# Retention attention and two MLPs on one core: q, k and v loaded in five transfers a chunk, and three moves on ScalarE in the first MLP

## The chip, the core and the metric

The kernel runs on one core of a Trainium2 chip. A core has TensorE (PE) for matrix products, VectorE (DVE), ScalarE (ACT) and GpSimd (POOL) for elementwise work, and SyncE (SP), which here issues nearly all DMAs. The engines run side by side and wait for each other through semaphores; each engine takes its own instructions strictly in the order of the program. The metric is the device time of one execution in microseconds (us).

## The reference

Attention with decay over 2 batches and 8 heads of 768 positions by 64, in blocks, then two MLPs over the 1536 tokens. Everything is float32.

```
for b in range(nb):                                   # blocks of the sequence
    intra = (qb @ kb.T) * Dmask                       # lam**(i-j), j <= i
    out   = intra @ vb + (qb * lam_pow) @ kv_state
    kv_state = lam_block * kv_state + (kb * rev_pow).T @ vb
x = out as (1536 tokens, 512)
h = x @ w_in1 ; x = (h * cos(h)) @ w_out1             # w_in: 512 x 2048, w_out: 2048 x 512
h = x @ w_in2 ; out = (h * sigmoid(h)) @ w_out2
```

## The kernel before

All instructions stand in the order in which the code below is written; there is no scheduler. Four stages follow each other, and on PE they join without a break.

**Attention** works on 6 chunks (c) of 128 positions. Per chunk, `load_qkv` brings k, q and v of all 16 (batch, head) pairs into a tile of 128 partitions, one position a partition, 64 numbers (256 B) a head. Two heads at a time are transposed on PE (`transposed`, tiles `pt`), copied out by ACT (`kT`, `qT`), multiplied into scores (`psc`), masked by DVE with the table `dm` and multiplied with v (`pso`). In parallel k is decayed (`att_kdec`, `kd`, on POOL from chunk 1 on) for the state (`pkv`). For batch 1 the kernel wants an odd and an even head to stand in the other half of the 128 rows than for batch 0. Before, the load did this: batch 1 of k and q came in two strided transfers which put heads 1, 3, 5, 7 on even places and 0, 2, 4, 6 on odd ones. k and q tiles have 2 buffers, v has 3; chunk c+2 is requested while chunk c is worked on. Between them SP also loads the first weights.

**First MLP, `gemm_in_0`.** The tokens are split in a part A of 1024 tokens, computed by seven products (`product(A, 1)` to `product(A, 7)`, six matmuls each), and a part B of 512 tokens by a plain product (`plain`, twice 12 matmuls). 2048 hidden columns are done in 8 pairs j of 2 x 128. One pass of the loop over j holds, on PE in this order, products 1, 7, 6 and 2 of pair j, `plain(B, 0)` of pair j-1, product 5, `plain(B, 1)`, and products 3 and 4: 66 matmuls. Three PSUM banks of A are copied on the way by ACT: `copy_ab` (L462) after product 1 starts a second sum from the first, and product 6 needs it; `copy_u` (L469) saves the bank as `u2` after product 6 and as `u4` after product 5. Products 5 and 3 go on summing in the bank that `u2` and `u4` save, so product 3 can't start before the `u4` copy has read it.

The activation of a finished half (`source`) takes four steps: `act_n` on ACT (L485, number of turns), `act_s` on DVE (L494, remainder), `act_sin` on ACT (L501, the sine), `act_g` on DVE (L507, times h), and a store of the result to DRAM (`gd`) by SP. In pass j this is done for both halves of part A of pair j-1 (`old`) and for half 0 (the only one) of part B of pair j-1 (`Bq`).

The weights of pair j+1 are made ready in the same pass by tasks that are put into slots (j, 0), (j, 1) and (j, 2) of the loop. Weights come as 64-bit words in tiles `raw` (512 KB, 3 buffers). `rebias_w` (ACT, L109) reads one half of the words, `convert_w` (DVE, L118 and L119) the other; only after both is the buffer free and `load_next` has SP load the next piece into it. `sum_w` (POOL, L137, tiles `S`) forms sums of weight blocks, `split_plain` and `split_sums` split weights and sums into a rounded part (ACT, L124) and a rest (POOL, L125, `win`).

```
for i in range(2):
    put((j - 1, 0), lambda f=f + i: convert_w(0, f, 0), load_next)   # pair j, f = 2j
put((j - 1, 0), lambda j=j: sum_w(0, j, nc.gpsimd))
put((j - 1, 1 - early), lambda j=j: split_plain(0, j))
put((j - 1, 2 - early), lambda j=j: split_sums(0, j))
```

By this rule pass p converts pieces 2p+2 and 2p+3 and at once loads pieces 2p+5 and 2p+6; and pass p also rebiases pieces 2p+4 and 2p+5. The later of these two, 2p+5, is thus requested in the pass that rebiases it, behind its first `convert_w`.

**After the loop** PE goes on with `gemm_out`, which reads the stored `gd` back (`load_half`, `load_g`), splits it (`prepare_half`, `prepare`: ACT L124 `gh`, POOL L125 `gl`) and multiplies it with the second weights, `wout`. The second MLP repeats the pattern; the change does not touch it.

Of the kernel before, what the change touches and what calls it, by code (L numbers as in the profile page):

```python
# [8 lines left out]
F32 = mybir.dt.float32  # L9
# [31 lines left out]
def tile_decay_attention__two_mlps(  # L41
# [158 lines left out]
    ps_s, ps_o = (psum_up.enter_context(tc.tile_pool(name=n, bufs=1, space=PSUM)) for n in ("ps_s", "ps_o"))  # L200
    half = [slice(e * C, (e + 1) * C) for e in range(2)]

    ident = ap_c.tile([P, P], F32, name="ident")
    lamb = ap_c.tile([P, P], F32, name="lamb")[:, 0:H]
    dm = ap_c.tile([P, H, P], F32, name="dm")
    qp = ap_c.tile([P, B, NP, P], F32, name="qp")

    def scan(out, step, first):
        nc.vector.tensor_tensor_scan(out=out, data0=step, data1=first, initial=0.0, op0=ALU.mult, op1=ALU.add)

    def table_dm():
        step = stage.tile([P, H, P], F32, tag="raw", name="step")
        nc.vector.tensor_copy(step, lamb[:, :, None].to_broadcast([P, H, P]))
        nc.vector.memset(step[:, :, 0:1], 0.0)
        scan(*(t.rearrange("p h i -> p (h i)") for t in (dm, step, diag)))

    def table_qp():
        first, step = both[:, 0], both[:, 1]
        by_s = lamb.rearrange("p (s y) -> p y s", y=2)
        for y in range(2):  # L220
            for b in range(B):
                lam_y = by_s[half[y], y ^ b]
# [24 lines left out]
    def transposed(c, part, pt, b):  # L247
        for s in range(NP):
            nc.tensor.transpose(
                pt[:, b, s, :], qkv[c, part][:, b, 2 * s:2 * s + 2, :].rearrange("p h d -> p (h d)"), ident  # L250
            )
# [33 lines left out]
    def att_kdec(c):  # L285
        if c == SC - 1:
            return
        t = ap_k.tile([P, B, H, D], F32, tag="kd", name="kd")
        engine = nc.gpsimd if c else nc.vector
        engine.tensor_tensor(  # L290
            out=t[:, 0], in0=qkv[c, "k"][:, 0], in1=dm[:, :, P - 1:P].to_broadcast([P, H, D]), op=ALU.mult
        )
        for y in range(2):
            engine.tensor_tensor(
                out=t[:, 1, y::2], in0=qkv[c, "k"][:, 1, y::2], in1=dm[:, 1 - y::2, P - 1:P].to_broadcast([P, NP, D]), op=ALU.mult
            )
        kd[c] = t

    def att_kv(c, pool, tag):
        if c == SC - 1:  # L300
            return
        ps = pool.tile([P, B, NP, D], F32, tag=tag, name="pkv")
        kt, vt = kd.pop(c), qkv[c, "v"]
        for b in range(B):
            for s in range(NP):
                for r in range(2):
                    nc.tensor.matmul(ps[half[r], b, s, :], kt[:, b, 2 * s + r, :], vt[:, b, 2 * s + (b ^ r), :], start=True, stop=True)
        pkv[c] = ps

    def att_state(c):  # L310
# [13 lines left out]
    def att_scores(c, b, pool, tag):  # L324
        (qT, _), kT = tr[c, "q"], tr[c, "k"]
        if b == 0:
            at[c] = ap_2.tile([P, B, 2, NP, P], F32, tag="at", name="at", bufs=1)
        ps = [pool.tile([P, NP, P], F32, tag=tag, name="psc", bufs=3) for _ in range(2)]
        for s in range(NP):
            for r in range(2):  # L330
                nc.tensor.matmul(ps[r][:, s, :], kT[half[r], b, s, :], qT[half[r], b, s, :], start=True, stop=True)
        for r in range(2):
            nc.vector.tensor_tensor(out=at[c][:, b, r], in0=ps[r], in1=dm[:, (b ^ r)::2, :], op=ALU.mult)

    def att_inter(c, pool, tag):
        ps = pool.tile([P, B, NP, P], F32, tag=tag, name="pso")
        po[c] = ps
        _, qd = tr[c, "q"]
        if c == 0:
            return  # L340
        st = state.pop(c)
        for s in range(NP):
            for e in range(2):
                for b in range(B):
                    r = half[b ^ e]
                    nc.tensor.matmul(ps[half[e], b, s, :], st[r, b, s, :], qd[r, b, s, :], start=s == 0, stop=False, skip_group_check=True)

# [113 lines left out]
    def copy_ab(Q):  # L461
        nc.scalar.copy(Q.banks["b"], Q.banks["a"])  # L462
# [50 lines left out]
    def gemm_in_0(tasks):  # L513


        def task(j, i):
            for x in tasks.get((j, i), []):
                x()

        old = quads_a[0]  # L520
        for j in range(1, FP):
            A, Bq = quads_a[j], quads_b[j - 1]
            if j > 1:
                product(A, 1)
# [48 lines left out]
        act_sin(Bq, 0)  # L573
        act_g(Bq, 0)
        gemm_out(0, 0, 1, (0, 1))
        task(FP, 1)
        prepare(0, 0, 2)
# [244 lines left out]
                send(2, m)  # L822

    with tc.manual_schedule():
        nc.scalar.dma_start(out=lamb, in_=lam.partition_broadcast(P))
        load_qkv(0, "k")
        load_qkv(0, "q", nc.scalar)
        load_qkv(0, "v")
# [131 lines left out]
        for L in range(2):  # L960
            tasks = {}
            if L == 0:
                for j in range(2, FP):
                    f = 2 * j
                    if j > 2:
                        put((j - 2, 2), *(lambda f=f + i: rebias_w(0, f, 0) for i in range(2)))
                        for i in range(2):
                            put((j - 1, 0), lambda f=f + i: convert_w(0, f, 0), load_next)
                        put((j - 1, 0), lambda j=j: sum_w(0, j, nc.gpsimd))
                    early = j == 2  # L970
                    put((j - 1, 1 - early), lambda j=j: split_plain(0, j))
                    put((j - 1, 2 - early), lambda j=j: split_sums(0, j))
# [70 lines left out]
```

## Time and profile before

| | |
|---|---|
| median of 3 runs | 570.6 us (570.12 to 571.87) |
| the profiled execution | 570.55 us, of which the span in the trace is 568.8 us |
| PE busy | 555.7 us, 98% of the span |
| DVE, ACT, POOL busy | 353.4, 294.4, 337.3 us |
| granted PE clock | 0.999 of full speed |
| DMA | 97.02 MB, mean 171 GB/s |

PE is busy nearly all the time, so 13.1 us of the span are PE's idle time, and what matters is which waits PE has and where. 1.75 us lie outside the span. Times below are microseconds from the start of the span.

### The profile page before, as it was taken

To read this page: it belongs to the slowest core of one execution; us is meant where nothing else is said; L and a number is where in the kernel's file an instruction comes from. 1 tells how busy PE (TensorE), PEld (TensorE's weight loads), DVE (VectorE), ACT (ScalarE), POOL (GpSimd) and SP (SyncE) were. 2 spreads that over 40 slices of the span, in tenths; PEclk is the share of its full clock that TensorE was granted. 3 is DMA by queue.
4 is the path that set the end of the run, shared out by engine and by line. 5 is a ranking of instruction groups with operands and counts; after the bars stand their busy time and mean duration, and the time that the engine had idled before them with its cause. 6 is when DMAs were issued, how large, how long until landed. Compare 5 with 4: busy or idle time off the path is not lost.

```text
span 568.8 us, 8373 instructions
## 1 busy us (share of the span) xinstructions
PE 555.7 (98%) x3168; PEld 461.4 (81%) x3168; DVE 353.4 (62%) x365; ACT 294.4 (52%) x440; POOL 337.3 (59%) x251
## 2 busy tenths in 40 slices
PE   7999999999999999999999999999999999999997
PEld 5878788777778688888888889888888888888885
DVE  6688876677669699900897446666866899102001
ACT  5567486667777655411842476556657555101220
POOL 3688355444455799950575067556727799901441
PEclk9999999999999999999999999999999999999999
DMA  8999235554437976650332045555558986205501
GB/s 196 209 228 260 60 127 186 184 181 154 138 154 271 358 260 227 233 169 1 115 109 74 2 154 196 184 186 178 211 193 307 359 253 184 75 0 176 195 1 74
DMA packets 79656, 97.02 MB, mean 171 GB/s; under 512 B 40704, under 2 KB 57088, under 8 KB 79616
## 3 DMA queue, kind: packets, MB, share of 16 engines
q1 hardware_dynamic: 77376, 95.96, 51.9%
q10 hardware_dynamic: 2240, 0.53, 0.4%
q8 instruction: 25, 0.41, 0.3%
q14 instruction: 15, 0.12, 0.1%
HBM read 68.16 MB, written 28.31 MB: 170 GB/s over the span
## 4 chain that ended last, share of the span: by engine, by line
PE 74%; DVE 6%; ACT 5%; POOL 5%; DMA 4%; issue 4%; SPq 1%; ACTq 0%; POOLq 0%; DVEq 0%
PE cab L705 38%; PE cab L432 18%; PE d L705 7%; PE d L432 6%; DMA raw<-in_moe_w_in_dram 2%; DVE s L494 2%; DVE s L507 1%; POOL gl L125 1%; ACT w L109 1%; POOL S L137 1%; ACT s L485 1%; POOL xal L398 1%; PE pso L353 1%; PE cab L448 1%; DMA raw<-in_moe_w_out_dram 1%
## 5 line engine op out<-in xcount | busy, mean ns | idle before, releaser
L125 POOL TENSOR_TENSOR gl<-gf,gh 128x512 fp32r<-128x512 f32 (+1 forms) x68 | 127.4, 1881 | 87.3 <-ACT gh L124 59.1
L705 PE MATMUL cab<-gh,wout 128*128 128x512 f32 x320 | 98.6, 389 | 0.0
L705 PE MATMUL cab<-wout,gh 128*128 128x512 f32 x320 | 98.5, 389 | 0.0
L119 DVE SCALAR_TENSOR_TENSOR w<-w,sb 128x512 uint32<-128x512 uint32 x64 | 90.1, 1408 | 8.1 <-ACT w L109 1.7
L432 PE MATMUL cab<-xah,win 128*128 128x512 f32 x320 | 87.3, 394 | 3.3 <-ACT cab L462 3.3
L124 ACT CAST gh<-gf 128x512 fp32r<-128x512 f32 (+1 forms) x68 | 53.4, 792 | 65.1 <-DMA out_dram<-o 38.7
L432 PEld LDWEIGHTS cab<-xah,win 128*128 128x128 f32 x320 | 58.6, 188 | 17.1 <-ACT cab L462 5.8
L137 POOL TENSOR_TENSOR S<-w 128x256 f32<-128x256 f32 x26 | 27.2, 1048 | 73.2 <-DVE w L119 73.2
L705 PEld LDWEIGHTS cab<-gh,wout 128*128 128x128 f32 x320 | 60.1, 188 | 12.6
L705 PEld LDWEIGHTS cab<-wout,gh 128*128 128x128 f32 x320 | 59.9, 188 | 12.3
L125 POOL TENSOR_TENSOR wout<-w,wout 128x512 fp32r<-128x512 f32 x32 | 52.4, 1643 | 22.9 <-ACT wout L124 22.9
L705 PE MATMUL cab<-wout,gl 128*128 128x512 f32 x160 | 62.4, 390 | 0.0
L705 PE MATMUL cab<-gl,wout 128*128 128x512 f32 x160 | 62.2, 389 | 0.0
L118 DVE TENSOR_SCALAR sb<-raw 128x512 uint32<-128x512 uint32 x64 | 59.4, 928 | 3.1 <-DMA raw<-in_moe_w_out_dram 2.1
L432 PE MATMUL cab<-xal,win 128*128 128x512 f32 x160 | 49.4, 390 | 0.0
L780 DVE COPY o<-cab 128x512 f32<-128x512 f32 x10 | 6.8, 691 | 68.4 <-PE cab L705 63.8
L469 ACT COPY u<-cab 128x512 f32<-128x512 f32 (+1 forms) x48 | 24.7, 514 | 39.2 <-PE cab L432 39.1
L109 ACT ACTIVATE w<-raw 128x512 f32<-128x512 f32 x64 | 41.8, 668 | 5.7 <-POOL wout L125 3.6
L125 POOL TENSOR_TENSOR win<-w,win 128x512 fp32r<-128x512 f32 (+1 forms) x32 | 39.4, 1252 | 3.0 <-ACT win L124 3.0
L124 ACT CAST wout<-w 128x512 fp32r<-128x512 f32 x32 | 19.7, 620 | 39.1 <-DVE w L119 39.1
L125 POOL TENSOR_TENSOR win<-S,win 128x512 fp32r<-128x512 f32 x26 | 36.7, 1433 | 3.4 <-ACT win L124 3.4
L507 DVE TENSOR_TENSOR s<-cab,s 128x1024 f32<-128x1024 f32 (+1 forms) x32 | 34.7, 1084 | 5.0 <-ACT s L489 3.6
(126 smaller groups left out, 983.5 us busy)
## 6 DMA issues: line engine op xcount, KB each, us to landing
gf<-gd SPq DMA_DIRECT2D x45, 512.0 KB, 4.3
gd<-s SPq DMA_DIRECT2D x40, 512.0 KB, 2.9
raw<-in_moe_w_in_dram SPq DMA_DIRECT2D x32, 512.0 KB, 4.4
raw<-in_moe_w_out_dram SPq DMA_DIRECT2D x32, 512.0 KB, 4.2
gd<-s SPq DMA_DIRECT2D x16, 256.0 KB, 2.1
v<-in_v_dram SPq DMA_DIRECT2D x12, 256.0 KB, 5.2
out_dram<-o SPq DMA_DIRECT2D x12, 256.0 KB, 2.2
k<-in_k_dram SPq DMA_DIRECT2D x6, 256.0 KB, 5.0
```

The lines of the kernel that those rows point to most:

```text
L109: nc.scalar.activation(w, raw[piece][:, :, 1].bitcast(F32), AF.Prelu, scale=2.0**-112, alpha=-(2.0**32))
L118: nc.vector.tensor_scalar(out=sb, in0=r[:, :, 0], scalar1=2.0**-29, scalar2=7.0, op0=ALU.mult, op1=ALU.min)
L119: nc.vector.scalar_tensor_tensor(out=w, in0=w, scalar=3, in1=sb, op0=ALU.logical_shift_left, op1=ALU.bitwise_or)
L124: nc.scalar.copy(hi, of)
L125: (engine or nc.gpsimd).tensor_tensor(out=lo, in0=of, in1=hi.bitcast(F32), op=ALU.subtract)
L137: engine.tensor_tensor(out=s[:, i], in0=x, in1=y, op=op)
L432: nc.tensor.matmul(Q.banks[bank], w[:, part, wu, kt * P:(kt + 1) * P], x[:, xu, kt, :], start=start and m == 0 and kt == 0, stop=m == 2 an ...
L469: nc.scalar.copy(t, Q.banks["b"])
L494: nc.vector.scalar_tensor_tensor(out=t.bitcast(F32), in0=source(Q, i), scalar=1.0 / (2.0 * math.pi), in1=t, op0=ALU.mult, op1=ALU.subtract)
L507: nc.vector.tensor_tensor(out=t, in0=source(Q, i), in1=t, op=ALU.mult)
L705: nc.tensor.matmul(y[m], x, z, start=f == 0 and n == 0, stop=f == FT - 1 and n == 2)
L780: nc.vector.tensor_copy(o, ys[1, b][2 + m])
```

## The change

Four edits, of which the first touches several functions.

1. `load_qkv`: k, q and v come with their heads in the natural order, all 16 in one transfer (128 x 16 x 64) instead of two or three. So that batch 1 still finds its heads in the other half, pairs of batch 1 begin one head later: heads 1-2, 3-4, 5-6 and 7-0. For the last pair, head 0 of batch 1 is loaded a second time (128 x 64, 32 KB) behind head 7, for k and for q. A chunk has 5 transfers in place of 8; in chunk 0 the large ones are split by batch. `head` and `place` tell which head stands where; `dm` and `lamb` get a ninth entry that repeats the first (one small DVE copy and one small ACT copy at the start); `att_kdec` does two operations in place of three.
2. `finish_b`: the sine of part B and its `act_g` are issued behind `product(A, 1)` and `copy_ab(A)` of the next pass, not ahead of them.
3. The `rebias_w` tasks go from slot (j-2, 2) to (j-2, 1), which is ahead of the `u4` copy.
4. Behind the loop, the fourth `prepare_half` is issued right behind the third.

```diff
@@ load_qkv
-            t = pool.tile([P, B, H, D], F32, tag=part, name=part, bufs=3 if part == "v" else 2)
-            src = [{"q": q, "k": k, "v": v}[part][b, :, r, :].rearrange("h p d -> p h d") for b in range(B)]
+            t = pool.tile([P, 2 * H if part == "v" else 2 * H + 2, D], F32, tag=part, name=part, bufs=3 if part == "v" else 2)
+            x = {"q": q, "k": k, "v": v}[part].rearrange("b h s d -> s (b h) d")[r]
             eng = engine or nc.sync
-            if part == "v":
-                for b in range(B):
-                    eng.dma_start(out=t[:, b], in_=src[b])
-            else:
-                eng.dma_start(out=t[:, 0], in_=src[0])
-                for y in range(2):
-                    eng.dma_start(out=t[:, 1, y::2, :], in_=src[1][:, 1 - y::2, :])
+            for h in (slice(0, H), slice(H, 2 * H)) if c == 0 else (slice(0, 2 * H),):
+                eng.dma_start(out=t[:, h], in_=x[:, h])
+            if part != "v":
+                eng.dma_start(out=t[:, 2 * H], in_=x[:, H])
...
@@ transposed
+            h = b * (H + 1) + 2 * s
+            nc.tensor.transpose(pt[:, b, s, :], t[:, h:h + 2, :].rearrange("p h d -> p (h d)"), ident)
...
@@ gemm_in_0
+        def finish_b(Q):
+            act_sin(Q, 0)
+            act_g(Q, 0)
+
...
             if j > 1:
                 product(A, 1)
                 copy_ab(A)
+                finish_b(quads_b[j - 2])
                 product(A, 7)
...
             act_s(A, 0)
-            act_sin(Bq, 0)
-            act_g(Bq, 0)
             old = A
+        finish_b(Bq)
...
         prepare_half(0, 1, 0)
+        prepare_half(0, 1, 1)
         act_n(Bq, 0)
...
         gemm_out(0, 0, 0, (0, 1))
-        prepare_half(0, 1, 1)
...
@@ the tasks of gemm_in_0
-                        put((j - 2, 2), *(lambda f=f + i: rebias_w(0, f, 0) for i in range(2)))
+                        put((j - 2, 1), *(lambda f=f + i: rebias_w(0, f, 0) for i in range(2)))
```

On ACT, in pass 3 of the loop, the instructions stood so before (`win<-w` is `split_plain`, `win<-S` is `split_sums`, `w<-raw` is `rebias_w` of pieces 10 and 11, the two `s<-cab` are `act_n` of part B and of part A, `s<-s` is the sine of part B, and the last row is `copy_ab` of pass 4):

```order
L124 CAST win_1328<-w_1224 128x512
L124 CAST win_1328<-w_1226 128x512
L469 COPY u4_1339<-cab_1262 128x512
L124 CAST win_1328<-S_1307 128x512 x2
L109 ACTIVATE w_1347<-raw_1182 128x512
L109 ACTIVATE w_1349<-raw_1300 128x512
L485 ACTIVATE s_1363<-cab_1315,consts_75 128x1024
L485 ACTIVATE s_1372<-cab_1262,consts_75 128x1024
L501 ACTIVATE s_1363<-s_1363,consts_75 128x1024
L462 COPY cab_1385<-cab_1385 128x512
```

After the change the same pass reads:

```order
L124 CAST win_1310<-w_1192 128x512
L124 CAST win_1310<-w_1194 128x512
L109 ACTIVATE w_1315<-raw_1164 128x512
L109 ACTIVATE w_1317<-raw_1282 128x512
L473 COPY u4_1325<-cab_1241 128x512
L124 CAST win_1310<-S_1289 128x512 x2
L489 ACTIVATE s_1345<-cab_1297,consts_75 128x1024
L489 ACTIVATE s_1354<-cab_1241,consts_75 128x1024
L466 COPY cab_1364<-cab_1364 128x512
L505 ACTIVATE s_1345<-s_1345,consts_75 128x1024
```

The two `rebias_w` moved from behind the `u4` copy and `split_sums` to ahead of both, and `copy_ab` and the sine of part B changed places. The rows stand so in passes 2 to 5; in pass 6 only the second of the two moves is there.

On SP, the loads of one chunk (chunk 3) and of the weight piece between them were, before:

```order
L242 DMA k_270<-in_k_dram 128x8x64
L244 DMA k_270<-in_k_dram 128x4x64 x2
L242 DMA q_285<-in_q_dram 128x8x64
L244 DMA q_285<-in_q_dram 128x4x64 x2
L91 DMA raw_289<-in_moe_w_in_dram 128x4x256
L240 DMA v_291<-in_v_dram 128x8x64 x2
```

After it they are:

```order
L248 DMA k_264<-in_k_dram 128x16x64
L250 DMA k_264<-in_k_dram 128x64
L248 DMA q_278<-in_q_dram 128x16x64
L250 DMA q_278<-in_q_dram 128x64
L91 DMA raw_281<-in_moe_w_in_dram 128x4x256
L248 DMA v_283<-in_v_dram 128x16x64
```

Eight issues became five, and nothing moved past them.

On POOL, behind the loop, the split of the stored activations (`gl`, four halves and then whole ones) and of the second weights (`wout`) stood so before (from the third half on):

```order
L125 TENSOR_TENSOR gl_1898<-gf_1827,gh_1897 128x512
L125 TENSOR_TENSOR wout_1929<-w_1821,wout_1929 128x512
L125 TENSOR_TENSOR gl_1898<-gf_1829,gh_1897 128x512
L125 TENSOR_TENSOR wout_1958<-w_1846,wout_1958 128x512
L125 TENSOR_TENSOR gl_1898<-gf_1922,gh_1897 128x1024
```

After it:

```order
L125 TENSOR_TENSOR gl_1880<-gf_1809,gh_1879 128x512
L125 TENSOR_TENSOR gl_1880<-gf_1811,gh_1879 128x512
L125 TENSOR_TENSOR wout_1913<-w_1803,wout_1913 128x512
L125 TENSOR_TENSOR wout_1940<-w_1828,wout_1940 128x512
L125 TENSOR_TENSOR gl_1880<-gf_1904,gh_1879 128x1024
```

The fourth half moved ahead of one `wout`; the whole ones behind it kept their place.

## Rows read from the trace of the kernel before

**Rows 1.** Waits of PE: engine, line, whom for: us in total, times, longest.
```profile
PE cab L432 <- ACT cab L462: 3.6, 6, 0.8
```

**Rows 2.** Timeline of PE, product 6 of passes 2, 4 and 7: start, us, instruction.
```profile
85.67 1.07 PE L432 MATMUL cab<-xah,win 128*128 128x512 f32 x4
...
117.04 1.19 PE L432 MATMUL cab<-xah,win 128*128 128x512 f32 x4 [0.75 <-ACT cab L462]
...
165.14 1.19 PE L432 MATMUL cab<-xah,win 128*128 128x512 f32 x4 [0.78 <-ACT cab L462]
```

**Rows 3.** Timeline of PE, pass 5: product 1, products 3 and 1 (pass 6).
```profile
129.41 1.07 PE L432 MATMUL cab<-xah,win 128*128 128x512 f32 x4
130.32 0.62 PE L432 MATMUL cab<-xal,win 128*128 128x512 f32 x2
...
142.73 1.07 PE L432 MATMUL cab<-xah,win 128*128 128x512 f32 x4
...
145.45 1.07 PE L432 MATMUL cab<-xah,win 128*128 128x512 f32 x4
```

**Rows 4.** Timeline of ACT in the same pass.
```profile
131.39 1.15 ACT L501 ACTIVATE s<-s,consts 128x1024 f32<-128x1024 f32 x1 [0.29 <-DVE s L494]
132.44 0.58 ACT L462 COPY cab<-cab 128x512 f32<-128x512 f32 x1
...
140.26 0.59 ACT L469 COPY u<-cab 128x512 f32<-128x512 f32 x1 [0.72 <-PE cab L432]
142.86 1.14 ACT L124 CAST win<-S 128x512 fp32r<-128x512 f32 x2 [2.01 <-POOL S L137]
143.90 1.22 ACT L109 ACTIVATE w<-raw 128x512 f32<-128x512 f32 x2
```

**Rows 5.** Timeline of DVE in the same pass.
```profile
130.12 1.23 DVE L494 SCALAR_TENSOR_TENSOR s<-cab,s 128x1024 f32<-128x1024 f32 x1 [4.59 <-ACT s L485]
...
133.00 1.22 DVE L507 TENSOR_TENSOR s<-cab,s 128x1024 f32<-128x1024 f32 x1
...
136.41 0.42 DVE L118 TENSOR_SCALAR sb<-raw 128x512 uint32<-128x512 uint32 x1
```

**Rows 6.** Timeline of SP in the same pass: the weight load behind that conversion.
```profile
136.96 0.37 SPq L91 DMA_DIRECT2D raw<-in_moe_w_in_dram  x1
```

**Rows 7.** DMA issues, first weight load of passes 2 to 5: KB, us to landing.
```profile
raw<-in_moe_w_in_dram SPq DMA_DIRECT2D x1, 512.0 KB, 6.1
raw<-in_moe_w_in_dram SPq DMA_DIRECT2D x1, 512.0 KB, 5.7
raw<-in_moe_w_in_dram SPq DMA_DIRECT2D x1, 512.0 KB, 5.8
raw<-in_moe_w_in_dram SPq DMA_DIRECT2D x1, 512.0 KB, 5.0
```

**Rows 8.** DMA issues from 68.5 to 69 us: a weight load with nothing else under way.
```profile
raw<-in_moe_w_in_dram SPq DMA_DIRECT2D x1, 512.0 KB, 3.7
```

**Rows 9.** Timeline of PE, chunks 3 and 4 of the attention.
```profile
33.95 1.52 PE L307 MATMUL pkv<-v,kd 128*64 128x64 f32 x32 [0.21 <-DMA v<-in_v_dram]
...
40.48 0.63 PE L249 MATMUL pt<-ident,q 128*128 128x128 f32 x4 [0.93 <-DMA q<-in_q_dram]
```

**Rows 10.** Busy time by stretch: us, PE, PEld, DVE, ACT, POOL, PEclk, DMA share, GB/s.
```profile
10.00:12.00 2.00, 1.98 (x45) 1.72 (x42) 1.91 (x2) 0.76 (x1) 0.00 (x1) 1.00 1.08 245
```

**Rows 11.** Timeline of PE behind the loop.
```profile
189.36 0.50 PE L705 MATMUL d<-gl,wout 128*128 128x512 f32 x1 [1.34 <-POOL gl L125]
...
199.06 0.39 PE L705 MATMUL cab<-gl,wout 128*128 128x512 f32 x1
```

**Rows 12.** Timeline of POOL behind the loop.
```profile
184.33 1.82 POOL L125 TENSOR_TENSOR gl<-gf,gh 128x512 fp32r<-128x512 f32 x1 [0.61 <-ACT gh L124]
...
188.04 1.26 POOL L125 TENSOR_TENSOR gl<-gf,gh 128x512 fp32r<-128x512 f32 x1
...
196.24 2.47 POOL L125 TENSOR_TENSOR gl<-gf,gh 128x1024 fp32r<-128x1024 f32 x1 [0.80 <-ACT gh L124]
```

More of the change, by code (lines that the diff above doesn't have):

```diff
@@ L201, in tile_decay_attention__two_mlps, with head, place @@
     half = [slice(e * C, (e + 1) * C) for e in range(2)]
+    def head(b, s, r):
+        return (2 * s + r + b) % H
+    def place(b, h):
+        return (h - b) % H // 2, (h + b) % 2
     ident = ap_c.tile([P, P], F32, name="ident")
-    lamb = ap_c.tile([P, P], F32, name="lamb")[:, 0:H]
-    dm = ap_c.tile([P, H, P], F32, name="dm")
+    lamb = ap_c.tile([P, P], F32, name="lamb")[:, 0:H + 1]
+    dm = ap_c.tile([P, H + 1, P], F32, name="dm")
     qp = ap_c.tile([P, B, NP, P], F32, name="qp")
@@ L212, in table_dm @@
         step = stage.tile([P, H, P], F32, tag="raw", name="step")
-        nc.vector.tensor_copy(step, lamb[:, :, None].to_broadcast([P, H, P]))
+        nc.vector.tensor_copy(step, lamb[:, 0:H, None].to_broadcast([P, H, P]))
         nc.vector.memset(step[:, :, 0:1], 0.0)
-        scan(*(t.rearrange("p h i -> p (h i)") for t in (dm, step, diag)))
+        scan(*(t.rearrange("p h i -> p (h i)") for t in (dm[:, 0:H], step, diag)))
+        nc.vector.tensor_copy(dm[:, H], dm[:, 0])
     def table_qp():
         first, step = both[:, 0], both[:, 1]
-        by_s = lamb.rearrange("p (s y) -> p y s", y=2)
+        nc.scalar.copy(lamb[:, H:], lamb[:, 0:1])
         for y in range(2):
             for b in range(B):
-                lam_y = by_s[half[y], y ^ b]
+                lam_y = lamb[half[y], y + b:y + b + H - 1:2]
                 nc.scalar.copy(first[half[y], b, :, 0], lam_y)
@@ L234, in load_qkv @@
             pool = ap_2 if part == "v" else ap_k
[L235 to L236 removed]
+            t = pool.tile([P, 2 * H if part == "v" else 2 * H + 2, D], F32, tag=part, name=part, bufs=3 if part == "v" else 2)
+            x = {"q": q, "k": k, "v": v}[part].rearrange("b h s d -> s (b h) d")[r]
             eng = engine or nc.sync
[L238 to L244 removed]
+            for h in (slice(0, H), slice(H, 2 * H)) if c == 0 else (slice(0, 2 * H),):
+                eng.dma_start(out=t[:, h], in_=x[:, h])
+            if part != "v":
+                eng.dma_start(out=t[:, 2 * H], in_=x[:, H])
             qkv[c, part] = t
     def transposed(c, part, pt, b):
+        t = qkv[c, part]
         for s in range(NP):
[L249 to L251 removed]
+            h = b * (H + 1) + 2 * s
+            nc.tensor.transpose(pt[:, b, s, :], t[:, h:h + 2, :].rearrange("p h d -> p (h d)"), ident)
     def att_kT(c, pt):
@@ L288, in att_kdec @@
         t = ap_k.tile([P, B, H, D], F32, tag="kd", name="kd")
[L289 to L295, printed above, removed]
+        for b in range(B):
+            (nc.gpsimd if c else nc.vector).tensor_tensor(
+                out=t[:, b], in0=qkv[c, "k"][:, b * H:(b + 1) * H], in1=dm[:, 0:H, P - 1:P].to_broadcast([P, H, D]), op=ALU.mult
             )
@@ L306, in att_kv @@
                 for r in range(2):
-                    nc.tensor.matmul(ps[half[r], b, s, :], kt[:, b, 2 * s + r, :], vt[:, b, 2 * s + (b ^ r), :], start=True, stop=True)
+                    h = head(b, s, r)
+                    nc.tensor.matmul(ps[half[r], b, s, :], kt[:, b, h, :], vt[:, b * H + h, :], start=True, stop=True)
         pkv[c] = ps
@@ L332, in att_scores @@
         for r in range(2):
-            nc.vector.tensor_tensor(out=at[c][:, b, r], in0=ps[r], in1=dm[:, (b ^ r)::2, :], op=ALU.mult)
+            nc.vector.tensor_tensor(out=at[c][:, b, r], in0=ps[r], in1=dm[:, b + r:b + r + H - 1:2, :], op=ALU.mult)
     def att_inter(c, pool, tag):
@@ L344, in att_inter @@
                 for b in range(B):
-                    r = half[b ^ e]
-                    nc.tensor.matmul(ps[half[e], b, s, :], st[r, b, s, :], qd[r, b, s, :], start=s == 0, stop=False, skip_group_check=True)
+                    u, r = place(b, 2 * s + e)
+                    nc.tensor.matmul(ps[half[e], b, s, :], st[half[r], b, u, :], qd[half[r], b, u, :], start=s == 0, stop=False, skip_group_check=True)
     def att_intra(c):
@@ L352, in att_intra @@
                 for e in range(2):
+                    u, r = place(b, 2 * s + e)
                     nc.tensor.matmul(
-                        ps[half[e], b, s, :], vt[:, b, 2 * s + e, :], a[:, b, e ^ b, s, :],
+                        ps[half[e], b, s, :], vt[:, b * H + 2 * s + e, :], a[:, b, r, u, :],
                         start=c == 0 and s == 0, stop=True, skip_group_check=True,
@@ L571, in gemm_in_0 @@
         gemm_out(0, 0, 0, (0, 1))
-        prepare_half(0, 1, 1)
-        act_sin(Bq, 0)
-        act_g(Bq, 0)
+        finish_b(Bq)
         gemm_out(0, 0, 1, (0, 1))
@@ L824, in tile_decay_attention__two_mlps @@
     with tc.manual_schedule():
-        nc.scalar.dma_start(out=lamb, in_=lam.partition_broadcast(P))
+        nc.scalar.dma_start(out=lamb[:, 0:H], in_=lam.partition_broadcast(P))
         load_qkv(0, "k")
```

## The prediction

> **What bounds the kernel now.** I read the busy shares first: PE works 98% of the span at a granted clock of 0.999, so time can only come from PE's few waits or go into new ones. The list of PE's waits shows where those are, the timeline around each shows what PE waits for, and the order of the changed program shows what will stand ahead of that.
>
> In the first MLP a pass holds 66 matmuls. Products 3 and 4 are 12 of them and take from 142.73 to 145.45, 2.72 us or 0.227 each [rows 3], so a pass without waits takes 66 x 0.227 = 14.96 us. It takes more: product 6 of pass 2 starts at 85.67 and that of pass 7 at 165.14 [rows 2], five passes in 79.47, 15.9 each. The difference, 4.7 us over the five, sits at product 6, which waits for `copy_ab` on ACT: PE lists six such waits with 3.6 us [rows 1], and each leaves PE with slower first matmuls or unlisted gaps behind it, the remaining 1.1. In pass 5 the reason is visible: ACT does the sine of part B at 131.39, released by DVE, and `copy_ab` only behind it, at 132.44 [rows 4], though product 1 had ended at 130.32 + 0.62 = 130.94 [rows 3]. That is the wait the second edit addresses. Elsewhere PE is idle behind the loop, 1.34 us for `gl` [rows 11], and twice in the attention, 0.21 and 0.93 us for loads [rows 9].
>
> **The change part by part.**
>
> *The copy ahead of the sine (edit 2).* `copy_ab` (0.58) can start when product 1 ends, 1.53 us after its start. Product 7 covers it on PE with 6 x 0.227 = 1.36. So the wait at product 6 goes, and by itself this is worth up to 4.7 us over five passes, if nothing later in the pass becomes the limit. The sine comes 0.58 later.
>
> *The rebias ahead of the `u4` copy (edit 3).* Here something does become the limit. In pass 5 two `rebias_w` take 1.22 us at 143.90, behind the `u4` copy at 140.26 [rows 4]; after the change they stand directly ahead of that copy, and in passes 2 to 5 the second of them reads the piece whose load is requested in the same pass, because there are three raw buffers. DVE starts that pass's first conversion, which frees the buffer, at 136.41 [rows 5]; SP issues the load at 136.96, 0.55 later [rows 6]; these loads land 6.1, 5.7, 5.8 and 5.0 us after their issue [rows 7]. For pass 5, 136.96 + 5.0 = 141.96. Before the change that was early enough: the rebias began at 143.90, after a wait of 2.01 for POOL's sums [rows 4]. Now ACT, which takes its instructions in order, stands at the rebias until 141.96 and only then reaches the `u4` copy, which ran at 140.26. PE's product 3 can't start before that copy, since it goes on in the same bank. PE's wait so moves from product 6 to product 3. Queued behind on ACT are also `split_sums` and both `act_n`, whose users on DVE come in the next pass.
>
> The delay doesn't stay within a pass, for the next load depends on the next product 1. The circle, each step with its duration in pass 5: product 1 from start to end 1.53 [rows 3]; `copy_ab` 0.58 and the sine 1.15 [rows 4]; DVE from `act_g` of part B at 133.00 to the conversion at 136.41, 3.41 [rows 5]; to the issue of the load 0.55 [rows 6]; the landing L; the second rebias 0.61, half of 1.22, and the `u4` copy 0.59 [rows 4]; then products 3 and 4, 2.72 [rows 3]. For four hand-overs between engines I take 0.05 each, 0.2, my choice (131.35, the end of `act_s` in [rows 5], to the sine's start at 131.39 is 0.04). Together 11.34 + L. With the L of before, passes 2 to 5 take 17.4, 17.0, 17.1 and 16.3, or 67.9. Pass 6 has no rebias and only gains: 14.96. Five passes: 82.8 in place of 79.5, **+3.3 us**. The point from which the load is the limit at all is L = 14.96 - 11.34 = 3.6; the passes are as long as before on average at L = 4.9 (four passes of 16.1 and one of 14.96 make 79.5).
>
> So what L will be is the main question. A 512 KB weight load with nothing else under way landed in 3.7 us [rows 8]; that is the lower bound and gives no wait worth the name. The upper one is the longest of the four, 6.1, which in all four passes gives 4 x 17.44 + 14.96 = 84.7, +5.2. I take the four rows as they are, since the order on SP and on DVE is unchanged: the second load and the stores of results that share the engines with this one still stand at the same places next to it.
>
> For loads of this size the Trainium skill, "DMA: Bandwidth & Descriptors", section "Anatomy of one DMA — SWDGE (gpsimd) path", gives a fit of 2.0 us plus the bytes over 436 thousand a microsecond, for a DMA by itself on that path; my estimate from it for 512 KB is 3.2 us, by which the circle would be 14.5 and the edit would show no wait: 565.5. The rows contradict it here: 3.7 alone and 5.0 to 6.1 in the pass.
>
> *Behind the loop (edit 4).* The fourth `gl` half is done at 188.04 + 1.26 = 189.30, and PE gets it at 189.36 after 1.34 of idle time [rows 11, 12]. Issued right behind the third, which ends at 184.33 + 1.82 = 186.15, it would be done at about 187.4, which removes this wait. But the next limit stands close: a whole `gl` ends on POOL at 196.24 + 2.47 = 198.71 [rows 12], and PE takes up its product at 199.06 [rows 11]. Its chain is untouched, so all but 0.35 of what PE gains comes back as a wait there. I take **-0.4 us**; the bounds are 0 and -1.3. The `wout` that moves behind the fourth half has the slack of the halves that PE multiplies first.
>
> *Attention (edit 1).* The attention is as long as PE's work in it, with 1.14 us lost to loads [rows 9], so fewer issues are worth at most -1.1. Against that, k and q carry 2 x 32 KB more a chunk. Up to chunk 4's q, where PE already waits, these are 10 x 32 = 320 KB more, 1.3 us at the 245 GB/s of a filled stretch [rows 10], if all of it delays that load. Also, a chunk's first transposes, four in 0.63 [rows 9], now wait for 512 KB, not for the 256 KB of batch 0: with these 0.5 us the upper end is +1.8. Between -1.1 and +1.8 I take **+0.3**: the middle, for the transfers are requested two chunks ahead, which covers most of a delay. The two small copies for `dm` and `lamb` are on DVE and ACT while the first loads are under way, and the third `att_kdec` operation saved was not awaited by PE; I count both as nothing, and 0.2 us for the first chunk if they are not covered.
>
> Two rules of the Trainium skill speak to this edit, and against each other. "Perfetto Trace Analysis", section "DMA Optimizations", says that splitting a DMA may let part of the work start sooner where the DMA engines are mostly idle, by which merging is at the upper end, +1.8 and 575.2 in all; "DMA: Bandwidth & Descriptors", section "Rules for kernel authors", wants small transfers coalesced and 1 MiB or more in each, by which it is at the lower end, 572.3. PE's two waits, 0.2 and 0.9 us, are too short to decide between them.
>
> **Sum.** 570.55 (the profiled execution; the median is 570.6) + 3.3 - 0.4 + 0.3 = **573.7 us**.
>
> **The rivals.**
>
> *A: the loads land in time (faster).* If L is at most 3.6 in the new order, nothing replaces the wait at product 6 and the loop loses its 4.7 us: 570.55 - 4.7 - 0.4 + 0.3 = 565.8. For it: the lone load's 3.7, and in the new order all of pass p's stores may be out earlier relative to it. Against it: the four landings, of which none is under 5.0. A load would have to get 1.4 us faster with the same neighbours. It decides in the other direction from L = 4.9.
>
> *B: the two moves cancel.* With L about 4.5 to 5.0, a pass is 15.8 to 16.3 and the five are 78.3 to 80.3: 569.3 to 571.3, no change that can be told. Pass 5's 5.0 speaks for it, the other three against it.
>
> *C: the loop as forecast, and the attention pays in full*, +1.8 in place of +0.3: 575.2. For it speaks that PE waits for q already, so there is no slack at that place; against it, that the DMA engines have the whole chunk before to recover.
>
> **How the numbers follow.** What can be told from no change is 0.3%, 1.7 us. Chances: the forecast 0.48, A 0.17, B 0.2, C 0.15. The likeliest case by itself has 572.0 to 575.5. The range starts at 569.0, which takes in B and leaves out A, and ends at 576.5, which takes in C and a landing of 6.1 in every pass with some of the attention's price. Faster (under 568.9) is A: 0.17. Within 0.3% (568.9 to 572.3) is B and the lower edge of the forecast: 0.23. Slower: 0.60.
>
> **What the changed profile would show.** If I am right, PE's list of waits no longer has `cab` of product 6 behind `copy_ab`, but some four waits of 1.5 to 2.5 us at product 3 behind the `u4` copy, and ACT has as many waits for `raw` at L109. Product 6 comes 16.3 to 17.4 us apart in passes 2 to 5 and 15.0 from pass 6 to 7. `copy_ab` follows directly on product 1, ahead of the sine. Behind the loop the gap at `gl` 128x512 is gone and smaller ones stand at `gl` 128x1024. In the attention PE waits for q in chunk 4, by up to 2 us. I am wrong if ACT's rebias finds its `raw` there without a wait (then A), if loads of this line land in under 4.5 us, or if PE waits in the loop for something that is not on the circle, as POOL's sums.

## The result

The changed kernel takes 577.2 us (median) where the kernel before takes 570.4: the ratio is 1.0109, with an interval of 1.0078 to 1.0140. One of the four executions was slow (585.12 us, granted clock 0.991) and counts in the median but not in the ratio; the others took 576.24, 576.44 and 577.92. The direction was as forecast; the size, 6.8 us by the medians in place of 3.1, was not, and the median lies just above the range, which ends at 576.5. The profiled execution is the one of 577.92, with a span of 576.1, so its 7.3 us over the span of before (568.8) are what the trace can show.

PE does as many matmuls of the same kinds in the same order in both kernels, so the difference can be read off by stage. The first MLP begins at 53.23 before and 55.28 after: **+2.05** in the attention, where +0.3 was forecast. From there to product 6 of pass 7 (165.14 before [rows 2], 170.15 after) are 111.91 and 114.87: **+2.96** in the loop, forecast +3.3. From there to the start of PE's last matmul are 399.62 and 401.92: **+2.30** behind the loop, forecast -0.4.

PE's list of waits after the change (engine, line, whom for: us in total, times, longest) answers to [rows 1]:

```profile
PE cab L436 <- ACT u L473: 6.1, 4, 2.1
PE cab L712 <- POOL gl L125: 2.8, 2, 2.0
...
PE psc L334 <- DVE at L336: 1.1, 2, 1.0
PE pkv L310 <- DVE kd L296: 0.8, 1, 0.8
...
PE d L712 <- POOL gl L125: 0.4, 1, 0.4
PE cab L436 <- ACT cab L466: 0.3, 1, 0.3
```

The wait for `copy_ab` fell from 3.6 us to 0.3 (what is left stands in the second MLP, at 341 us, as it did before), and 6.1 us behind the `u4` copy took its place. Three other groups are new: `kd` in the first chunk, the masked scores `at` from DVE in the attention, and two waits at whole `gl` halves where there was none. PE's timeline shows where they stand:

```profile
11.84 1.29 PE L310 MATMUL pkv<-v,kd 128*64 128x64 f32 x32 [0.82 <-DVE kd L296]
...
49.14 1.16 PE L334 MATMUL psc<-qT,kT 64*128 64x128 f32 x14 [0.97 <-DVE at L336]
...
55.28 0.39 PE L432 MATMUL cab<-zeros 128*128 128x512 bf16 x1
...
99.47 1.21 PE L436 MATMUL cab<-xah,win 128*128 128x512 f32 x4 [2.06 <-ACT u L473]
...
105.08 1.07 PE L436 MATMUL cab<-xah,win 128*128 128x512 f32 x4
...
116.58 1.21 PE L436 MATMUL cab<-xah,win 128*128 128x512 f32 x4 [1.82 <-ACT u L473]
...
122.19 1.07 PE L436 MATMUL cab<-xah,win 128*128 128x512 f32 x4
...
170.15 1.19 PE L436 MATMUL cab<-xah,win 128*128 128x512 f32 x4
...
206.25 0.50 PE L712 MATMUL cab<-gl,wout 128*128 128x512 f32 x1 [1.96 <-POOL gl L125]
```

The rows at 105.08 and 122.19 are product 6 of passes 3 and 4: a pass of 17.11 us. ACT, in order of time, shows the waiting instruction in each of the three stages:

```profile
2.63 3.49 ACTq L250 DMA_DIRECT2D q<-in_q_dram  x1
6.16 1.28 ACT L847 ACT_TABLE_LOAD   x1 [6.16 <-issue]
...
98.28 0.66 ACT L109 ACTIVATE w<-raw 128x512 f32<-128x512 f32 x1 [3.07 <-DMA raw<-in_moe_w_in_dram]
98.84 0.57 ACT L473 COPY u<-cab 128x512 f32<-128x512 f32 x1
...
115.39 0.66 ACT L109 ACTIVATE w<-raw 128x512 f32<-128x512 f32 x1 [2.68 <-POOL S L137]
115.96 0.57 ACT L473 COPY u<-cab 128x512 f32<-128x512 f32 x1
...
201.89 0.68 ACT L109 ACTIVATE w<-raw 128x512 f32<-128x512 f32 x1 [2.60 <-DMA raw<-in_moe_w_out_dram]
202.47 1.99 ACT L124 CAST gh<-gf 128x1024 fp32r<-128x1024 f32 x2
```

In the loop the second `rebias_w` waits for its load and the `u4` copy follows at once. At 115.39 the trace names POOL, but the instruction doesn't read `S`; its piece had just landed. SP had issued two loads from 109.56 on,

```profile
109.56 1.58 SPq L91 DMA_DIRECT2D raw<-in_moe_w_in_dram  x2
```

and the first load of passes 2 to 5, then the load that ACT awaits at 201.89 (KB, us to landing), took this long:

```profile
raw<-in_moe_w_in_dram SPq DMA_DIRECT2D x1, 512.0 KB, 6.0
...
raw<-in_moe_w_in_dram SPq DMA_DIRECT2D x1, 512.0 KB, 5.8
...
raw<-in_moe_w_in_dram SPq DMA_DIRECT2D x1, 512.0 KB, 5.2
...
raw<-in_moe_w_in_dram SPq DMA_DIRECT2D x1, 512.0 KB, 5.0
...
raw<-in_moe_w_out_dram SPq DMA_DIRECT2D x1, 512.0 KB, 5.9
```

109.56 + 5.8 is 115.4, where the rebias starts. At the two other places the kernel before stood better. These are rows of its ACT, not shown so far:

```profile
1.20 0.45 ACTq L242 DMA_DIRECT2D q<-in_q_dram  x1
1.68 1.16 ACTq L244 DMA_DIRECT2D q<-in_q_dram  x2
2.88 1.28 ACT L840 ACT_TABLE_LOAD   x1 [2.88 <-issue]
...
194.55 0.67 ACT L109 ACTIVATE w<-raw 128x512 f32<-128x512 f32 x1 [0.80 <-DMA raw<-in_moe_w_out_dram]
```

In chunk 0, q goes out from ACT in three transfers in both kernels: 256, 128 and 128 KB before, 256, 256 and 32 KB after.

So three things were to be tested: that the load in the loop is in a circle with product 3, that one issue on ACT delays the first chunk, and that behind the loop the same kind of in-order wait (a `rebias_w` for a fresh load, with `gh` queued behind it) costs 2.3 us.

### The profile page after: what moved, and what is told of

It reads as the page before. It is cut to its first block, busy times and chain, and to the rows that moved or that the text cites. A ratio compares the mean times of both kernels' runs of the same rounds, so it can differ in the third digit from the quotient of the medians.

```text
span 576.1 us, 8344 instructions
## 1 busy us (share of the span) xinstructions
PE 558.9 (97%) x3168; PEld 463.4 (80%) x3168; DVE 347.3 (60%) x365; ACT 294.1 (51%) x441; POOL 337.0 (58%) x247
## 4 chain that ended last, share of the span: by engine, by line
PE 79%; DMA 6%; DVE 4%; issue 4%; ACT 3%; POOL 2%; SPq 0%; DVEq 0%; ACTq 0%; POOLq 0%
PE cab L712 36%; PE cab L436 20%; PE d L436 8%; PE d L712 7%; DMA raw<-in_moe_w_in_dram 4%; PE psc L334 2%; PE pso L357 2%; PE pt L257 2%; POOL gl L125 2%; DVE s L511 1%; PE cab L452 1%; ACT s L505 1%; PE pso L349 1%; DMA raw<-in_moe_w_out_dram 1%; ACT u L473 1%
## 5 line engine op out<-in xcount | busy, mean ns | idle before, releaser
L125 POOL TENSOR_TENSOR gl<-gf,gh 128x512 fp32r<-128x512 f32 (+1 forms) x68 | 129.7, 1913 | 88.7 <-ACT gh L124 60.5
L119 DVE SCALAR_TENSOR_TENSOR w<-w,sb 128x512 uint32<-128x512 uint32 x64 | 78.8, 1231 | 9.2 <-ACT w L109 2.2
L118 DVE TENSOR_SCALAR sb<-raw 128x512 uint32<-128x512 uint32 x64 | 65.1, 1017 | 4.4 <-DMA raw<-in_moe_w_out_dram 3.4
L125 POOL TENSOR_TENSOR wout<-w,wout 128x512 fp32r<-128x512 f32 x32 | 49.6, 1554 | 22.9 <-ACT wout L124 22.9
L712 PEld LDWEIGHTS cab<-gl,wout 128*128 128x128 f32 x160 | 30.0, 188 | 9.8 <-POOL gl L125 3.6
```

The costliest lines, as they stand in the source:

```text
L118: nc.vector.tensor_scalar(out=sb, in0=r[:, :, 0], scalar1=2.0**-29, scalar2=7.0, op0=ALU.mult, op1=ALU.min)
L119: nc.vector.scalar_tensor_tensor(out=w, in0=w, scalar=3, in1=sb, op0=ALU.logical_shift_left, op1=ALU.bitwise_or)
L125: (engine or nc.gpsimd).tensor_tensor(out=lo, in0=of, in1=hi.bitcast(F32), op=ALU.subtract)
L712: nc.tensor.matmul(y[m], x, z, start=f == 0 and n == 0, stop=f == FT - 1 and n == 2)
```

## The experiments

Each ran beside the kernel before (median 570.4 to 570.7). All 14 profiles by stage, in us: the start of the first MLP; from there to product 6 of pass 7; from there to the start of PE's last matmul; ACT's wait for `raw` at the seventh `w_out` piece; and the median of all executions. The stages of a row come from one execution, and executions of a kernel differ: the twelve of e4 took 569.9 to 574.5 us, the profiled ones of e3, e6 and e9 were the longest of theirs, those of e2 and e10 the shortest.

| kernel | attention | loop | behind it | ACT's wait | median |
|---|---|---|---|---|---|
| before | 53.23 | 111.91 | 399.62 | 0.80 | 570.4 |
| changed | 55.28 | 114.87 | 401.92 | 2.60 | 577.2 |
| e1 rebias back | 56.04 | 111.55 | 399.96 | 0.73 | 573.9 |
| e2 q0 on SP | 54.02 | 116.15 | 400.13 | 0.93 | 576.7 |
| e3 gl4 back | 54.49 | 115.13 | 404.39 | 3.78 | 578.8 |
| e4 split rebias | 55.24 | 109.32 | 401.52 | 2.27 | 572.2 |
| e5 loads alone | 55.14 | 111.87 | 402.07 | 3.54 | 574.8 |
| e6 copy + split | 53.69 | 109.32 | 402.07 | 2.97 | 569.5 |
| e7 gl4 alone | 53.14 | 111.87 | 399.42 | 0.77 | 570.3 |
| e8 e6 + gl4 | 52.81 | 109.32 | 402.31 | 3.26 | 569.8 |
| e9 changed, late piece | 54.47 | 119.28 | 399.39 | - | 576.3 |
| e10 e6, late piece | 52.51 | 109.33 | 400.00 | - | 568.5 |
| e11 e8, late piece | 52.54 | 109.30 | 399.55 | - | 567.7 |
| e12 changed, 3 repairs | 54.00 | 109.31 | 399.45 | - | 568.6 |

In e1, e2, e3 and e9 a stretch of half clock on PE stands in the profile as well (below): about 1.5 us in e1's attention and in e2's loop, as much behind the loop in e3, and twice that in e9's loop.

**e1, the rebias back.**

```diff
-put((j - 2, 1), *(lambda f=f + i: rebias_w(0, f, 0) for i in range(2)))
+put((j - 2, 2), *(lambda f=f + i: rebias_w(0, f, 0) for i in range(2)))
```

> The changed kernel with its third edit undone: both rebias_w stand in slot (j-2, 2) again, behind the u4 copy. Theory (the load of piece 2p+5 sits in a circle with product 3): the four waits of PE at product 3 (6.1 us) are gone, and ACT no longer waits for raw in the loop. The copy ahead of the sine alone is worth little, since the sine and with it DVE's conversions come later: a pass about 15.95 us, product 6 of pass 7 some 3.4 us earlier than in the changed kernel (which has 170.15), so at about 166.8, and 573 to 574 us in all. Rival (the wait at product 3 comes from something else on ACT, such as POOL's sums or the later sine): PE still waits at product 3 by more than 1 us a pass, and the time stays at 576 to 578.

It was 573.9 us (ratio 1.0061, 1.0037 to 1.0084), and the loop fell from 114.87 to 111.55. The wait behind `u4` is gone from PE's list, and a smaller one, for POOL's part of `win`, is there:

```profile
PE d L436 <- POOL win L125: 2.4, 4, 0.7
```

So the third edit cost the loop 3.3 us, near the theory's 3.4; the copy ahead of the sine alone is worth 0.36 on before, not the 4.7 that its wait had cost.

**e2, one transfer on another queue.**

```diff
-eng.dma_start(out=t[:, 2 * H], in_=x[:, H])
+nc.sync.dma_start(out=t[:, 2 * H], in_=x[:, H])
```

> The changed kernel with one transfer issued from another engine: in chunk 0, q's second copy of head 0 (128 x 64, 32 KB) goes out from SP, not from ACT. Theory (this issue held ACT for 3.49 us, and ACT's first activation, DVE's table dm and kd all stood behind it): ACT's table load starts at about 2.7 in place of 6.16, the dm scan on DVE at about 5.4 in place of 8.63, PE's pkv of chunk 0 at about 9.7 in place of 11.84, its wait for kd (0.82) is gone, and the time falls by 1.5 to 2.5 us, to 574 to 575.5. Rival (the extra bytes and the larger transfers delay the first chunk, whoever issues them): the first transposes and pkv stay late by about 2 us, and the time stays at 576 to 578.

ACT and PE went as the theory said:

```profile
2.64 1.28 ACT L847 ACT_TABLE_LOAD   x1 [2.64 <-issue]
```

```profile
9.26 0.69 PE L310 MATMUL pkv<-v,kd 128*64 128x64 f32 x16 [0.35 <-DMA v<-in_v_dram]
...
98.38 1.20 PE L436 MATMUL cab<-xah,win 128*128 128x512 f32 x4 [2.25 <-ACT u L473]
...
100.05 1.91 PE L436 MATMUL d<-xah,win 128*128 128x512 f32 x4
```

The table load starts at 2.64, the first `pkv` at 9.26 in place of 11.84, and its wait for `kd` is gone. But the time stayed at 576.7 (1.0114, 1.0092 to 1.0137), as the rival had it. Of the 2.6 us, 1.3 reach the first MLP, for PE then waits for loads again (1.5 us for q, 0.6 for v). And the loop took 116.15, with the same waits at product 3: the four matmuls at 100.05 took 1.91 us where others of their kind take 1.07. The table by stretches (us, busy PE, PEld, DVE, ACT, POOL, granted PE clock, DMA share, GB/s) shows why:

```profile
90.00:94.00 4.00, 4.00 (x20) 3.30 (x19) 3.74 (x6) 2.84 (x4) 1.15 (x1) 1.00 0.77 226
98.00:102.00 4.00, 3.62 (x11) 2.91 (x12) 1.92 (x2) 3.40 (x5) 3.57 (x3) 0.71 0.06 25
```

After 2.25 us without work PE was granted its lower level, 1.2 GHz, for part of the next stretch. The time alone would have spoken for the rival; the stages show that the theory's place is right and that most of its gain is lost elsewhere in this execution.

**e3, the fourth edit undone.**

```diff
 prepare_half(0, 1, 0)
-prepare_half(0, 1, 1)
 ...
 gemm_out(0, 0, 0, (0, 1))
+prepare_half(0, 1, 1)
```

> The changed kernel with its fourth edit undone: the fourth prepare_half stands behind the first gemm_out again. Theory (the fourth half on POOL right behind the third runs beside DVE's act_g of part A, which took 2.10 us in place of 1.23, and all behind it is later): act_g takes 1.2 to 1.4 us again, the stores, gf loads and the raw load behind them come 0.9 us sooner, PE waits 1 to 1.6 us at gl 128x512 but less at the two gl 128x1024 (2.8 us in the changed kernel): the time is 0 to 1.5 us lower. Rival A (those waits come from the weight load that lands 1.8 us later because of what else is under way, with or without the fourth edit): the waits at gl 128x1024 stay at 2 us or more, and the time is the same within 1 us. Rival B (the edit gains its 1.3 us): the time is 1 us higher.

578.8 us (1.0133, 1.0112 to 1.0155). The theory here was wrong: DVE's `act_g` took 2.11 us in this kernel too, and in e7, which has the fourth edit, 1.23. Rival A holds in part: ACT waited 3.78 us for the weight load, and PE waited 1.7 us at a whole `gl` half (2.0 at the longest in the changed kernel). The 1.3 us at the fourth half are back as well, as rival B needs. Why the time rose by more than 1 us is open: in the profile a stretch of half clock stands behind those waits, but two of the six executions took 578.5 and 578.6 us at a granted clock of 1.000.

**e4, one of two rebias_w back.**

```diff
-put((j - 2, 1), *(lambda f=f + i: rebias_w(0, f, 0) for i in range(2)))
+for i in range(2):
+    put((j - 2, 1 + i), lambda f=f + i: rebias_w(0, f, 0))
```

> The changed kernel with one rebias_w moved back: piece 2p+4 stays in slot (j-2, 1), piece 2p+5 goes to slot (j-2, 2), behind the u4 copy and split_sums. Theory (only the second of the two waits for its load, since the first's was requested a pass earlier): no wait of ACT for raw ahead of u4, none of PE at product 3, and the first rebias fills time in which ACT would wait for POOL's sums; passes of 15.0 to 15.5 us, product 6 of pass 7 at about 164 to 165 in place of 170.15, and 570.5 to 572.5 us in all. Rival (any rebias ahead of u4 holds it back): PE still waits at product 3 for half or more of the 6.1 us, and the time is 574 or more.

572.2 us (1.0026, 1.0008 to 1.0045). The largest of PE's waits behind the loop and in it are now:

```profile
PE cab L712 <- POOL gl L125: 2.4, 2, 1.6
...
PE d L436 <- POOL win L125: 0.8, 4, 0.2
```

No wait behind `u4`: it was the second rebias, the one with the fresh load. The loop takes 109.32, 2.6 less than before.

**e5, the loads alone** (the changed kernel with edits 2 to 4 undone).

> The kernel before with the first edit alone (q, k and v in five transfers a chunk). Theory (the attention term: ACT stands 3 to 3.5 us at the issue of q's second copy of head 0, and the first chunk is late by 2 us or more; later some of PE's old waits for loads disappear into that): ACT's table load starts at 5.5 to 6.5 in place of 2.88, the first matmul of the first MLP at 55 to 56 in place of 53.2, the loop as before, and 572 to 573.5 us. Rival (what is lost at the start is regained at PE's old waits for loads, and the 2 us belong to another edit): the first MLP begins within 0.7 us of before, and the time is 570 to 571.3.

574.8 us (1.0074, 1.0056 to 1.0091), more than either side had. The attention is late by 1.9, as expected; the loop is as before. The rest stands behind the loop, which this edit doesn't touch:

```profile
199.21 0.67 ACT L109 ACTIVATE w<-raw 128x512 f32<-128x512 f32 x1 [3.54 <-DMA raw<-in_moe_w_out_dram]
199.78 1.98 ACT L124 CAST gh<-gf 128x1024 fp32r<-128x1024 f32 x2
```

This is ACT, with the wait that the changed kernel has at this place (2.60 us there, 3.54 here), and PE waits 1.7 us at `gl` behind it.

**e6, copy and split rebias on the old loads.** Before with `finish_b` as in the change and the `put` of e4.

> The kernel before with the second edit (copy_ab ahead of part B's sine) and the first of the two rebias_w moved to slot (j-2, 1), the second left in slot (j-2, 2); loads and fourth prepare_half as before. Theory (no load in the circle, both waits gone): passes of 15.4 us as in the run that split the rebias, product 6 of pass 7 at 162.5 to 163 in place of 165.14, and 567.8 to 569 us, the best so far. Rival (what the loop gains is given back behind it, where gl on POOL and the weight loads are not sooner): product 6 of pass 7 as early, but PE waits 1.5 us or more at gl 128x1024, and the time is 569.8 to 571.

569.5 us (0.9972, 0.9960 to 0.9984). The loop is 109.32, as in e4, but behind it 402.07: the rival. In the profiled execution, the longest of the twelve (570.87), nearly all of the loop's 2.6 us is given back; the median keeps 1.2 of it.

**e7, the fourth edit alone on before.**

> The kernel before with the fourth edit alone (the fourth prepare_half right behind the third). Prediction's term: PE's wait at gl 128x512 goes from 1.34 us to 0.4 or less, 0.4 to 1.3 us come back as waits at gl 128x1024, -0.4 in all, 569.7 to 570.6. Rival A (DVE's act_g of part A beside it becomes 2.1 us long, the stores and loads behind it later by 0.9): the waits at gl 128x1024 are 1.5 us or more, and the time is 571 or more. Rival B (all of it is gained): no wait at gl 128x1024, 569.2.

570.3 us (1.0009, 0.9986 to 1.0032). The stage behind the loop got 0.2 us shorter; two waits of 1.1 us together at whole `gl` halves took the place of the 1.34. This is the prediction's term, in a kernel whose load came in time.

**e8, both.**

> The run with the second edit and the split rebias, plus the fourth edit: the whole change but for its loads and for one of two rebias_w. Theory: product 6 of pass 7 at 162.5 to 163, the wait at gl 128x512 0.4 or less, 567.5 to 568.8 us. Rival (behind the loop the supply of gl sets the end): 569.5 to 570.5, with waits at gl 128x1024 that take up what the loop and the fourth edit gained.

569.8 us (0.9983, 0.9971 to 0.9996), the rival again.

**e9 to e12, the late piece.** Behind the loop, the `rebias_w` of the seventh `w_out` piece is issued behind the next two `gh` casts; all of them are on ACT. e9 is the changed kernel with this edit, e10 is e6 with it and e11 is e8 with it; e12 is the changed kernel with this, e2's and e4's edits:

```diff
 for i, x in enumerate(out_tasks(L, f)):
-    put((0, max(f - 5, 0) + i), x)
+    put((0, max(f - 5, 0) + (i or (L, f) == (0, 6))), x)
```

> The changed kernel with one rebias_w behind the loop issued later: that of the first MLP's seventh w_out piece stands behind the gh casts of the fourth and fifth whole halves on ACT, not ahead of them. Theory (the 2 us lost behind the loop are ACT waiting 2.60 us for that piece's load, which landed 5.9 us after its issue in place of 4.06, with gh and so gl queued behind it): PE's wait of 1.96 us at gl 128x1024 goes, 1 to 2 us are gained, 574 to 575.7. Rival (POOL or the loads of gf make gl late): PE waits at gl 128x1024 as before, 576 to 577.5.

> The run with the second edit and the split rebias, and the same w_out rebias_w issued later. Theory: ACT's wait for raw ahead of gh (2.97 us) and PE's wait of 1.7 us at gl 128x1024 are gone, and what the loop gains reaches the end: 567 to 568.2 us, faster than the kernel before by 0.4 to 0.6%. Rival (the next limit stands close behind): a gain of under 0.6 us, 568.9 to 569.8.

> The same with the fourth edit too. Theory: with gh no longer behind that load, the 1.3 us at the fourth gl half are kept as well: 566 to 567.5 us. Rival (POOL is the limit: a gl of 128x1024 takes 2.4 to 2.6 us there): the fourth edit adds under 0.4 us to the run without it.

> The changed kernel with all its four edits and three repairs: q's second copy of head 0 in chunk 0 issued from SP, the second of the two rebias_w back in slot (j-2, 2), the w_out rebias_w later. Theory: the loop gains 2.5 us on before, the tail 1 us, and the attention still costs 0.5 to 1 us: 567.5 to 569 us. What it is above the run with the fourth edit and the old loads is what the five transfers cost when ACT isn't held. Rival (the loads' cost isn't in that one issue): 570 or more, with the first MLP's begin 1.5 us or more later than before.

e9 took 576.3 us (1.0097, 1.0072 to 1.0123): PE's wait of 1.96 is gone and the stage is at 399.39, 2.5 less than in the changed kernel; its profile loses about 3 us in the loop to two stretches of half clock, each behind a wait at product 3. But its load landed in 4.2 us (e11's too, e10's in 5.0), and with a load in time the stage is as short without this edit, so e9 doesn't test it. e10 took 568.5 (0.9956, 0.9939 to 0.9973) and e11 567.7 (0.9952, 0.9935 to 0.9968), both a little above what was expected; with the late piece the fourth edit is worth 0.45 us of the stage and 0.8 of the median, more than the rival had and less than the theory's 1.3. e12 took 568.6 (0.9962, 0.9949 to 0.9976). This is the run that tests the late piece:

```profile
191.18 1.22 ACT L109 ACTIVATE w<-raw 128x512 f32<-128x512 f32 x2
192.30 1.03 ACT L124 CAST gh<-gf 128x1024 fp32r<-128x1024 f32 x1
```

These are ACT's rows. The load in question was issued at 189.05 and landed 6.2 us later, longer than in the changed kernel (5.9), but `gh` no longer stands behind it, and the stage takes 399.45.

## Why the prediction was wrong

**The loop: right, in mechanism and size.** PE's wait moved from product 6 to product 3, four times, and the circle gives the passes: 11.34 + 5.8 = 17.1 for pass 3, where 17.11 was measured; 16.5 for pass 4 (landing 5.2), measured 16.49; 16.3 for pass 5 (5.0), measured 16.29. Pass 2, with 6.0, was to take 17.3 and took 17.36. The landings were close to those of before, as assumed, and the sum was 0.3 us too high. Two slips in its working change nothing: passes as long as before need a landing of 4.8, not 4.9 (11.34 + 4.8 = 16.1), and the 565.5 leaves out the attention's +0.3. By the Trainium skill, "DMA: Bandwidth & Descriptors", section "Anatomy of one DMA — SWDGE (gpsimd) path", the prediction's estimate for 512 KB was 3.2 us. That fit is for another path, DMAs that GpSimd issues; the loads here, which SP issues with other transfers under way, took 1.8 us or more longer. e1 and e4 show the cause by taking it away: without the load in the circle the wait is gone, and the move that leaves it out gains 2.6 us, in e4, e6, e8 and e10 to e12 alike.

**The attention: the term +0.3 failed, at the step that priced edit 1 by its added bytes at chunk 4 and left out what an issue costs the engine that makes it.** It counted the first chunk's extra work on ACT and DVE as nothing, or 0.2. But q's first chunk goes out from ACT. Its three transfers held ACT for 1.6 us together before; after, the first two took 1.39 and the third, of 32 KB, 3.49. ACT's table load, DVE's `dm` and `kd` and PE's first `pkv` all stood behind that: `pkv` starts at 11.84 in place of 9.64. Only 0.82 of this is the listed wait for `kd`, because in this execution PE's first matmuls were slow too (four at 6.35 took 1.91 us, 1.03 before); in e5 they weren't, and there the wait for `kd` is 1.34 and `pkv` starts at 11.72. PE was 2.7 us late at 15.8 and 0.7 at 41.7, since its old waits for loads were gone, the one for q in chunk 4 too, where the prediction expected up to 2 us. It lost 1.4 again in chunk 5, 0.97 of it waiting for DVE; at that place e6, e10 and e11 wait 0.7 with the old loads.

With the third transfer on SP (e2, e12) the first MLP starts at 54.0; with it on ACT, in five kernels, at 54.5 to 55.3, mean 54.9 (e1 left out for its half clock); with the old loads, in six, at 52.5 to 53.7, mean 53.0. By these means the issue on ACT costs 0.9 us and the rest of the edit 1.0, with a scatter nearly as large within each group. Whether this 1.0 comes from bytes or from the larger transfers wasn't separated; rival C, for both, had +1.8 in all. The sign is that of the Trainium skill, "Perfetto Trace Analysis", section "DMA Optimizations", by which splitting may let some work start sooner; but that rule speaks of DMA engines that are mostly idle, and here they were busy (DMA share 1.08 from 10 to 12 us [rows 10]), so no run here shows it at work.

**Behind the loop: the term -0.4 failed at "its chain is untouched".** The chain of a whole `gl` doesn't only hold its own `gf`, `gh` and POOL's work. Ahead of `gh` on ACT stands a `rebias_w` that waits for a load issued one step before. Before the change this wait was 0.80 us, and 399.62 was near the shortest that any run has (399.39). Where the load landed in 4.0 to 4.2 us, with the wait still in `gh`'s way, the stage took 399.4 to 400.1 (before, e1, e2, e7). Where it landed in 5.6 to 7.1 and ACT waited 1.5 us or more longer, it took 1.9 us or more longer: 401.5 to 402.3 in five kernels, 404.4 in e3 with its half clock. With the wait out of `gh`'s way it is 399.45 in e12 with a landing of 6.2, and 400.0 in e10 with 5.0. The term by itself was right in its sign and near its size (e7: -0.2).

**What stays open** is why that load lands 4.0 us after its issue in some profiles and up to 7.1 in others. No single edit sorts them: e5, with the loads alone, is late, e6 too, without them; e1, with loads, copy and fourth edit, is in time. Nor do the transfers around it: in e1 and e12 the loads of `gf` and the store of `gd` next to it were issued within 0.1 us of the same distance, and it landed in 4.0 and 6.2. With one trace a kernel, it isn't known either whether the late load belongs to the kernel or to the execution; two executions of the changed kernel without a trace were 1.5 and 1.7 us shorter than the profiled one. So the +2.3 is shown for the profiled execution, and how often the changed kernel pays it is not.

## What to carry to other kernels

Before moving an instruction forward on an in-order engine, look up when each of its operands is requested, not only who writes it: a task whose load is issued in the same pass turns its engine's queue, and all that stands behind it, into a wait for the DMA. Split such a group by that criterion; here, with the copy moved too, taking one of two instructions forward gained 2.6 us and taking both lost 3. When transfers are merged or added, go through the issues of each engine, the first ones above all, and read the total by stages: a correct repair (e2) can leave the time as it was.

## What was not expected of the hardware

One DMA issue of 32 KB held ACT for 3.49 us in the changed kernel (3.03 to 3.49 in the six kernels that issue it there), as the fourth on ACT's queue, behind the small one of `lamb` and two of 256 KB, which took 0.45 and 1.39. The kernel before has a fourth issue on that queue too, behind less, and its third and fourth together took 1.16. In e2 the same transfer, as the fourth on SP's queue, took 0.43. SP can be held as well: in the changed kernel, an issue of the same 32 KB for k took 2.74. The rows of SP, of e2 and then of the changed kernel:

```profile
2.64 0.43 SPq L250 DMA_DIRECT2D q<-in_q_dram  x1
```

```profile
15.05 2.74 SPq L250 DMA_DIRECT2D k<-in_k_dram  x1
```

What decides how long an issue holds its engine was not tried.

PE waits of about 2 us were followed by half clock in some executions and not in others: the granted clock was 0.71 from 98 to 102 us in e2, behind a wait of 2.25, and 0.61 in e9 in the same stretch, but 1.00 in the changed kernel's profile behind one of 2.06. Where it came it cost about 1.5 us, nearly as much as the wait. Shorter waits in a row came before it too: in e1 PE worked 0.74 us from 10 to 12 us, with waits of at most 1.1, and from 12 to 14 the granted clock was 0.70; in e5 it worked 0.61 us in the same two and the clock stayed at 1.00. The kernel before waits at most 0.8 us at one place in its loop [rows 1], and its clock stayed at 0.999.
